# Output product of a gated MLP by Strassen's method, in float32 split into two parts

## The chip, the cores and the metric

The kernel runs on one core of a Trainium2 chip. The core has five engines that work side by side and wait for one another on semaphores: TensorE (PE in the profile, with PEld for its weight loads), VectorE (DVE), ScalarE (ACT), GpSimd (POOL) and SyncE (SP), which here only issues DMAs. TensorE reads SBUF and writes PSUM; DVE and ACT read PSUM and bring results back to SBUF. The metric is the device time of one execution in microseconds (us), as the median of several runs. The host lays out the arrays before and after; this isn't timed.

## The reference

Eight batches of 576 tokens with 8 heads of 64 go through attention in chunks of 64 tokens, and then through a gated MLP with a product along the tokens:

```python
scores = scale * np.matmul(q_c, k_c.transpose(0, 1, 2, 4, 3))   # per batch, head and chunk: 64 x 64
attn = np.exp(scores - np.max(scores, axis=-1, keepdims=True))
attn = attn / (np.sum(attn, axis=-1, keepdims=True) + 1e-09)
x = np.matmul(attn, v_c)                    # with the heads side by side: [8, 576, 512]
h = gelu_tanh(x @ w_in)                     # [8, 576, 1024]
u, v = h[..., :512], h[..., 512:]
v_n = (v - mu) / np.sqrt(var + 1e-06) * g_ln
v_s = np.einsum('ts,bsd->btd', w_sg, v_n) + b_sg[None, :, None]
out = x + (u * v_s) @ w_out                 # w_out: [512, 512]
```

All arrays are float32, w_in and w_out float64 in the host's arrays.

## The kernel before, in words

Every large product is made of three matmuls in place of one: each operand is split into a high part (rounded to fp32r by a copy on ACT) and a low part (the difference, on DVE), and low x high, high x low and high x high are added in one PSUM bank. `split` (L92) makes the two parts; all its copies stand on L94 and all its subtractions on L97.

The program runs attention over 36 tiles of 128 tokens and the MLP over 8 batches of 576. A batch has four stages of units on PE:

- v units (L448, four or five): 12 matmuls of 512 columns each, then gelu on ACT, statistics and normalisation on DVE, and a power on POOL. A fifth unit in even batches takes the 64 odd tokens of two batches. The results lie in the tile `v`.
- u units (L487, four): 24 matmuls of 288 columns, gelu, into the tile `u2`.
- s units (L505, four): the product along the tokens, 28 matmuls; its result times `u2` gives the tile `gt` (L518), which is split into `gh` and `gl`.
- o units (L527, four): 24 matmuls of 288 columns with `w_out`: four blocks of 128 along the depth, three matmuls each, two banks of 288 tokens. DVE adds `xf`, the attention's output (L545), and SP stores `ot` (L546).

Attention has three steps for a tile or a pair: S (scores, L304, with the softmax on DVE, ACT and POOL), T (transposition on DVE with copies on ACT and DVE, L366) and O (product with v, L390, after which `keep`, L423, splits the result into `xh` and `xl` and copies it to `xf`).

The order of the code is written out by hand: `START` (L45) for the first two batches, with a letter and a number for each step, and `SLOTS` (L59) for the later ones, where "8:S78" puts the scores of the tiles 7 and 8 behind the unit with index 8 of a batch. In `START`, L, W and w (and X, x) load and convert w_in, A loads q, k and v up to a tile, Y loads and converts an eighth of w_out (`o_w`, L215, eight steps on ACT and DVE), P and Q are S and O for a pair, G and g load and split w_sg, and D only keeps PE busy. The framework places semaphores and storage. It keeps the code's order as a priority, and puts a later instruction ahead on an engine when the earlier one isn't ready by its estimate.

Storage that matters: PSUM has two banks in `banks` (scores, and early transpositions) and three tiles `pm` of two banks each, which all units and the attention's output share (L455 and others). SBUF has four places `qkv_t` for q, k and v of a tile (L289), which `o_w` uses for staging too; four places `tmp` for `hs`, `blocks`, `gt` and `ot`; one `u2` and one `v`. A tile's load waits until a place is free: q and k in one DMA, v in four DMAs of 64 KB from tile 5 on (L297 to L301).

Of the kernel before, what the change touches and what calls it, by code (L numbers as in the profile page):

```python
# [80 lines left out]
def block_attention_gated_mlp(ctx: ExitStack, tc: tile.TileContext, qkv, w_in, w_out, w_sg, g_ln, b_sg, out):  # L81
# [133 lines left out]
    def o_w(et, half):  # L215
        nonlocal wout_h, wout_l
        if wout_h is None:
            wout_h, wout_l = (w_out_tile(i).rearrange("p (k e) -> p k e", k=KT) for i in range(2))
# [423 lines left out]
```

## Time and profile before

| what | value |
|---|---|
| three runs, median | 515.13 us (514.95 to 515.40) |
| span of the profiled execution | 513.4 us |
| instructions | 12458 |
| mean granted TensorE clock | 0.996 |
| DMA | 46.58 MB, mean 91 GB/s |
| o units, matmuls (L537) | 512 with `gh`, 256 with `gl` |
| waits of PE after 92 us, by the table of waits | none |

The page shows busy time per engine, the span in 40 slices, and the chain of work that ended last: followed back from the last instruction, at each step to what released it. "Idle before" is the time an engine stood before an instruction, with what ended it. PE's busy time rests on modelled ends of matmuls, so its starts are the safer thing to read. In the answers by line, "x32 | 24.1, 755 | 40.3 <-PE pm L514" means 32 instructions, 24.1 us busy, 755 ns for one, and 40.3 us idle before them, mostly until PE's L514 was done. In a timeline the first two columns are the start and the length in us.

### The profile page before, as it was taken

What the parts mean: (1) busy time and instruction counts of PE and PEld (TensorE: products, weight loads), DVE (VectorE), ACT (ScalarE), POOL (GpSimd) and SP (SyncE); (2) the same over time, 40 slices, a digit from 0 to 9 for tenths busy, and PEclk for the clock granted to TensorE, in tenths of its full rate; (3) what the DMA queues carried; (4) which work ended last, traced back from release to release, by engine and by line L of the source; (5) the groups of instructions that cost most, each with busy time, mean ns of one, the idle gap of its engine ahead of it and who ended that gap; (6) DMA issues with size and microseconds to landing.
All of it is one profiled execution on the core that took longest, in us unless ns stands there. A gap on an engine that the chain in (4) does not pass through costs nothing.

```text
span 513.4 us, 12458 instructions
## 1 busy us (share of the span) xinstructions
PE 497.4 (97%) x5278; PEld 461.4 (90%) x5278; DVE 336.9 (66%) x704; ACT 274.3 (53%) x509; POOL 73.7 (14%) x75
## 2 busy tenths in 40 slices
PE   4989999899999999999999999999999999999997
PEld 4577799799999899998999899998999899998996
DVE  6888759986867866577465676578456685536042
ACT  5788667854435775355643766345644666334210
POOL 0123200020110321013100141013100140102000
PEclk9999999899999999999999999999999999999999
DMA  8866001216338404060406204060406300020002
GB/s 333 301 190 196 0 1 43 83 39 178 95 121 234 118 1 126 24 193 2 124 10 184 87 0 126 24 193 2 124 1 193 87 0 3 17 78 0 1 1 92
DMA packets 49595, 46.58 MB, mean 91 GB/s; under 512 B 35202, under 2 KB 39554, under 8 KB 49540
## 3 DMA queue, kind: packets, MB, share of 16 engines
q1 hardware_dynamic: 49540, 45.80, 29.4%
q8 instruction: 41, 0.67, 0.6%
q14 instruction: 14, 0.11, 0.1%
HBM read 36.34 MB, written 9.44 MB: 89 GB/s over the span
## 4 chain that ended last, share of the span: by engine, by line
PE 83%; DVE 7%; ACT 5%; POOL 2%; issue 2%; DMA 1%; DVEq 0%; POOLq 0%; ACTq 0%
PE pm L514 21%; PE pm L537 19%; PE pm L494 19%; PE pm L457 17%; PE pm L415 3%; PE banks L329 3%; POOL sm L466 1%; PE pm L582 1%; DVE nmax L340 1%; DMA wsg<-w_in 1%; ACT ptT L385 1%; ACT ptT L380 1%; POOL xl L97 1%; DVE wsg L133 0%; ACT pt L349 0%
## 5 line engine op out<-in xcount | busy, mean ns | idle before, releaser
L514 PE MATMUL pm<-wsg,v 128*128 128x288 f32 x768 | 108.0, 296 | 0.0
L514 PEld LDWEIGHTS pm<-wsg,v 128*128 128x128 f32 x768 | 103.9, 189 | 0.4
L537 PE MATMUL pm<-gh,wout 128*128 128x288 f32 x512 | 92.3, 297 | 0.0
L537 PEld LDWEIGHTS pm<-gh,wout 128*128 128x128 f32 x512 | 76.1, 189 | 0.5
L363 POOL TENSOR_TENSOR pt<-pt,den 128x512 f32<-128x512 f32 x28 | 30.7, 1111 | 225.3 <-DVE den L362 150.3
L466 POOL TENSOR_TENSOR sm<-sm,neg_half 128x1 f32<-128x1 f32 x36 | 36.3, 1007 | 160.5 <-DVE sm L465 120.2
L494 PE MATMUL pm<-xh,win_l 128*128 128x288 f32 x256 | 55.5, 298 | 1.0 <-ACT win_l L179 1.0
L537 PE MATMUL pm<-gl,wout 128*128 128x288 f32 x256 | 55.5, 296 | 0.0
L94 ACT CAST gh<-gt 128x576 fp32r<-128x576 f32 x32 | 21.5, 673 | 62.8 <-DVE gt L518 62.8
L494 PE MATMUL pm<-xh,win_h 128*128 128x288 f32 x256 | 55.0, 296 | 0.0
L494 PE MATMUL pm<-xl,win_h 128*128 128x288 f32 x256 | 55.0, 296 | 0.0
L457 PE MATMUL pm<-win_h,xl 128*128 128x512 f32 x128 | 52.0, 406 | 0.0
L457 PE MATMUL pm<-win_l,xh 128*128 128x512 f32 x128 | 51.2, 400 | 0.0
L457 PE MATMUL pm<-win_h,xh 128*128 128x512 f32 x128 | 51.1, 399 | 0.0
L518 DVE TENSOR_TENSOR gt<-pm,u 128x576 f32<-128x576 f32 x32 | 24.1, 755 | 40.3 <-PE pm L514 40.3
L545 DVE TENSOR_TENSOR ot<-pm,xf 128x576 f32<-128x576 f32 (+1 forms) x33 | 24.1, 732 | 29.8 <-PE pm L537 29.8
L494 PEld LDWEIGHTS pm<-xh,win_l 128*128 128x128 f32 x256 | 41.4, 188 | 2.4 <-ACT win_l L179 1.4
L537 PEld LDWEIGHTS pm<-gl,wout 128*128 128x128 f32 x256 | 41.5, 189 | 0.0
L494 PEld LDWEIGHTS pm<-xl,win_h 128*128 128x128 f32 x256 | 41.0, 188 | 0.0
L494 PEld LDWEIGHTS pm<-xh,win_h 128*128 128x128 f32 x256 | 41.0, 188 | 0.0
L97 DVE TENSOR_TENSOR xl<-pm,xh 128x512 fp32r<-128x512 f32 (+1 forms) x34 | 21.7, 639 | 26.2 <-ACT xh L94 26.2
L463 DVE BATCH_NORM_STATS2 sm<-hs 128x6 f32<-128x512 f32 x36 | 24.7, 687 | 19.7 <-ACT hs L460 19.5
(121 smaller groups left out, 825.2 us busy)
## 6 DMA issues: line engine op xcount, KB each, us to landing
qkv_t<-qkv SPq DMA_DIRECT2D x32, 512.0 KB, 4.5
out_dram<-ot SPq DMA_DIRECT2D x31, 288.0 KB, 2.2
qkv_t<-qkv SPq DMA_DIRECT2D x124, 64.0 KB, 3.7
qkv_t<-qkv SPq DMA_DIRECT2D x3, 768.0 KB, 9.4
wsg<-w_in SPq DMA_DIRECT2D x4, 512.0 KB, 4.8
wout<-w_in SPq DMA_DIRECT2D x4, 512.0 KB
st<-w_out SPq DMA_DIRECT2D x8, 256.0 KB, 3.5
stage<-w_sg SPq DMA_DIRECT2D x5, 288.0 KB, 3.3
```

The source lines that it names most:

```text
L94: nc.scalar.copy(hi, src)
L97: lo_eng.tensor_tensor(lo, src, hi.bitcast(F32), op=ALU.subtract)
L329: nc.tensor.matmul(sc[o, c, h // 2, :], qt[r, 0, h, :], qt[r, 1, h, :], start=True, stop=True)
L363: (nc.gpsimd if t > last[1] else pick(f"n{t}")).tensor_tensor(pt, pt, den.unsqueeze(2).broadcast_to([P, H, D]), op=ALU.mult)
L457: nc.tensor.matmul(pv, a[:, kt, tok], c[:, kt, DH:], start=(i == 0), stop=(i == 11))
L463: nc.vector.bn_stats(st, h)
L466: nc.gpsimd.tensor_tensor(rs, rs, neg_half, op=ALU.pow)
L494: nc.tensor.matmul(pm[:, j, :HS], a[:, kt, dc], c[:, kt, j * HS : (j + 1) * HS], start=(i == 0), stop=(i == 11))
L514: nc.tensor.matmul(pm[:, j, :HS], a[:, dc], c[:, m, j * HS : (j + 1) * HS], start=(i == 0), stop=(i == len(ops) - 1))
L518: nc.vector.tensor_tensor(gt.rearrange("p (a c) -> p a c", a=2), pm[:, :, :HS], u2[0][:, dt, :].rearrange("p (a c) -> p a c", a=2), op=ALU ...
L537: nc.tensor.matmul(pm[:, j, :HS], a[:, kt, ec], c[:, kt, j * HS : (j + 1) * HS], start=(i == 0), stop=(i == len(ops) - 1),)
L545: nc.vector.tensor_tensor(ot[:, js], pm[:, js, :HS], res[:, js], op=ALU.add)
```

## The change

**Seven products for eight.** For batches 1 to 7 the output product is taken as one of 2x2 blocks: the weights W in blocks of 256 outputs by 256 deep, the gated input G (b11, b12, b21, b22 in the code) in blocks of 256 deep by 288 tokens. With Winograd's form of Strassen's method, S1 = W21 + W22, S2 = S1 - W11, S3 = W11 - W21, S4 = W12 - S2, and T1 = G12 - G11, T2 = G22 - T1, T3 = G22 - G12, T4 = G21 - T2, the products are

- P1 = W11 G11, P2 = W12 G21, P3 = S4 G22, P4 = W22 T4, P5 = S1 T1, P6 = S2 T2, P7 = S3 T3,
- out11 = P1 + P2, out12 = P1 + P6 + P5 + P3, out22 = P1 + P6 + P7 + P5, out21 = P1 + P6 + P7 + P4, each plus its part of x.

A product has 12 matmuls of 288 columns (two halves of outputs, two of depth, three for the split) into one `pm` tile. They run in the order 1, 5, 2, 6, 3, 7, 4. Products 1, 6, 7 and 4 add up in the same tile, 5 and 3 in a second; product 2 has a third. DVE reads a tile between two products. Product 4 comes behind the next batch's first v unit (in batch 7 it has a tile of its own and ends by halves).

```diff
+        if b >= FAST and dt == 1:
+            split(gh[b][:, 0], gl[b][:, 0], b11, nc.scalar, nc.vector)
+            nc.gpsimd.tensor_tensor(b11, b12, b11, op=ALU.subtract)
+            split(gh[b][:, 3], gl[b][:, 3], b11, nc.scalar, nc.vector)
+        if b >= FAST and dt == 3:
+            ts = gs[b] = mp.tile([P, 3, 2, 2, HS], F32R, name="ts", tag="v")
+            nc.vector.tensor_tensor(b11, b22, b11, op=ALU.subtract)
+            split(ts[:, 0, 0], ts[:, 0, 1], b11, nc.scalar, nc.vector)
+            nc.gpsimd.tensor_tensor(b12, b22, b12, op=ALU.subtract)
+            nc.gpsimd.tensor_tensor(b21, b21, b11, op=ALU.subtract)
...
+        if step == 0:
+            o["a"] = new()
+            product(b, 1, o["a"], True)
+            o["r1"] = o_part(o["a"], o_quarter(b, 0, 0))
+            split(ts[:, 1, 0], ts[:, 1, 1], b12, nc.scalar, nc.vector)
+            o["b"] = new()
+            product(b, 5, o["b"], True)
+            o["r5"] = o_part(o["b"], o_quarter(b, 1, 1))
+            split(ts[:, 2, 0], ts[:, 2, 1], b21, nc.scalar, nc.vector)
+        elif step == 1:
+            c = new()
+            product(b, 2, c, True)
+            o_store(b, 0, 0, o_part(c, o["r1"], o["r1"]))
+            product(b, 6, o["a"], False)
+            o["r2"] = o_part(o["a"], o_quarter(b, 0, 1))
+        elif step == 2:
+            product(b, 3, o["b"], False)
+            o_store(b, 0, 1, o_part(o["b"], o["r2"], o["r2"]))
+            product(b, 7, o["a"], False)
+            o_store(b, 1, 1, o_part(o["a"], o["r5"], o["r5"]))
+        elif b < B - 1:
+            product(b, 4, o["a"], False)
+            o_store(b, 1, 0, o_part(o["a"], o_quarter(b, 1, 0)))
+        else:
+            ot = o_part(o["a"], o_quarter(b, 1, 0))
+            d = new()
+            product(b, 4, d, True)
+            for e in range(2):
+                es = slice(e, e + 1)
+                o_part(d, ot, ot, es)
+                o_store(b, 1, 0, ot, es)
...
-        units += [(s_unit, i) for i in range(4)] + [(o_unit, i) for i in range(4)]
+        units += [(s_unit, i) for i in range(4)] + [(o_fast, i) for i in range(3)]
...
             f(b, k)
+            if i == 0:
+                o_fast(b - 1, 3)
```

`new` takes a `pm` tile, `product` issues the 12 matmuls, `o_part` is one DVE addition of 128x576 from PSUM, `o_store` one DMA. The gate's result is written back into `u2` in place of `gt`. In batch 0 the four o units stay, with blocks in another order in storage. T2 to T4 lie in `ts`, which takes the place of `v`.

**Weight sums.** Four new steps K0 to K3 in `START` make S1 to S4 once: `w_whole` adds a block's high and low part on POOL, further POOL additions and subtractions make the sums (eight POOL operations of 128x512 in all), and each sum is split on ACT and DVE. S1 takes the place of W21 after batch 0; the others lie in a new pair of tiles `wx`.

**Separate places for q, k and v.**

```diff
-            qt = att.tile([P, 3, H, D], F32, name="qkv_t", bufs=QKV_BUFS)
+        qks[t] = att.tile([P, 2, H, D], F32, name="qk", tag="qk")
+        nc.sync.dma_start(out=qks[t], in_=qkv[t, :, 0:2])
+        vt = vts[t] = att.tile([P, H, D], F32, name="av", tag="av")
...
     def scores(*tiles):
-        ahead(tiles[-1] + 2)
         att_scores(*tiles)
+        ahead(load_qk, tiles[-1] + 2)
+
+    def outputs(*tiles):
+        att_out(*tiles)
+        ahead(load_v, tiles[-1] + 2)
```

q and k have two places `qk`, v has two places `av`; tiles 2 and 4 lie in `wx`, and tile 3 in `u2` as before. q and k are loaded behind the scores that free their place, v behind the output that frees its own. `o_w` stages in `qk`. `START` gets the new steps and loads:

```diff
-L0 A0 A1 L1 S0 L2 T0 D11 A2 W0 A3 W1 L3 A4 S1 W2 S2 w0 w1 W3 T1 O0 w2 S3 O1 T2 w3 D14 O2 T3 S4 M0 v00 X0 O3 G0 T4 v01
-A8 O4 x0 X1 v02 x1 X2 v03 X3 v04 u00 x2 g0 g1 u01 x3 g2 g3 u02 P5 g4 u03 T5 s00 T6 P7 s01 Q5 s02 T7 T8 s03 Q7 v10 v11
-Y0 v12 Y1 v13 Y2 u10 Y3 u11 Y4 u12 Y5 Y6 u13 Y7 A10 s10 A12 s11 P9 s12 s13 T9 o00 T10 P11 o01 o02 o03 Q9 A14 T11 o10
-T12 o11 Q11 S13 A15 o12 T13 o13
+L0 A0 B0 A1 B1 L1 S0 L2 T0 D11 A2 W0 A3 W1 L3 A4 S1 W2 S2 w0 w1 W3 T1 O0 w2 S3 O1 T2 w3 D14 O2 T3 S4 M0 v00 X0 O3 G0 T4
+v01 A6 B6 O4 x0 X1 v02 x1 X2 v03 X3 v04 u00 x2 g0 g1 u01 x3 g2 g3 u02 P5 A8 g4 u03 T5 s00 T6 P7 s01 Q5 B8 s02 T7 T8
+s03 Q7 v10 v11 Y0 v12 Y1 v13 Y2 u10 Y3 u11 Y4 u12 Y5 Y6 u13 Y7 A10 B10 s10 K0 s11 K1 P9 A12 s12 K2 s13 T9 o00 T10 P11 A14
+o01 o02 o03 K3 Q9 B12 T11 o10 T12 o11 Q11 B14 S13 A15 o12 T13
```

More of the change, by code (lines that the diff above doesn't have):

```diff
@@ L217, in o_w @@
         if wout_h is None:
-            wout_h, wout_l = (w_out_tile(i).rearrange("p (k e) -> p k e", k=KT) for i in range(2))
+            wout_h, wout_l = (blocks_of(w_out_tile(i), 4) for i in range(2))
         n = 2 * P
-        cols, rows = slice(et * P, (et + 1) * P), slice(2 * half, 2 * half + 2)
-        st = att.tile([P, 3 * H * D], I32, name="st", tag="qkv_t", bufs=QKV_BUFS)[:, : 4 * n]
+        rows, blk, cols = slice(2 * half, 2 * half + 2), W_BLOCK[et // 2, half], slice(et % 2 * P, (et % 2 + 1) * P)
+        st = att.tile([P, 4 * n], I32, name="st", tag="qk")
         dst = st[:, : 2 * n].rearrange("p (k c) -> p k c", k=2)
@@ new lines, in s_unit, with g_split @@
+        nc.vector.tensor_tensor(row, pm[:, :, :HS], row, op=ALU.mult)
+        if dt == 0:
+            gh[b] = xp.tile([P, 4, 2, HS], F32R, name="gh", tag=f"big_{b % 2}")
+            gl[b] = xp.tile([P, 4, 2, HS], F32R, name="gl", tag=f"big_{b % 2}")
+        g_split(b, dt)
+    gs = {}
+    def g_split(b, dt):
+        k, two = dt % 2, slice(0, 4, 3) if dt < 2 else slice(1, 3)
+        g = u2[0]
+        row = g[:, dt, :].rearrange("p (a c) -> p a c", a=2)
+        if b < FAST or dt > 1:
+            split(gh[b][:, two, k, :], gl[b][:, two, k, :], row, nc.scalar, nc.vector)
+        b11, b12, b21, b22 = (g[:, 2 * i : 2 * i + 2, j * HS : (j + 1) * HS] for i in range(2) for j in range(2))
+        if b >= FAST and dt == 1:
[8 more added lines that the diff above has]
+            nc.gpsimd.tensor_tensor(b21, b21, b11, op=ALU.subtract)
@@ L541, in o_unit @@
         ot = tmp.tile([P, 2, HS], F32, name="ot", tag="tmp")
         res = xf[b][:, et, :].rearrange("p (a c) -> p a c", a=2)
[L543 to L554 removed]
+        nc.vector.tensor_tensor(ot, pm[:, :, :HS], res, op=ALU.add)
@@ new lines, in o_unit, with product @@
+        nc.sync.dma_start(out=out[b, et].rearrange("p (a c) -> p a c", a=2), in_=ot)
+    os = {}
+    def product(b, n, pm, first):
+        h, l, ts = gh[b], gl[b], gs[b]
+        wh, wl = wout_h, wout_l
+        (ah, al), (ch, cl) = {
+            1: ((wh[:, 0], wl[:, 0]), (h[:, 0], l[:, 0])),
+            2: ((wh[:, 1], wl[:, 1]), (h[:, 1], l[:, 1])),
+            3: ((wx[0][:, 2], wx[1][:, 2]), (h[:, 2], l[:, 2])),
+            4: ((wh[:, 2], wl[:, 2]), (ts[:, 2, 0], ts[:, 2, 1])),
+            5: ((wh[:, 3], wl[:, 3]), (h[:, 3], l[:, 3])),
+            6: ((wx[0][:, 0], wx[1][:, 0]), (ts[:, 0, 0], ts[:, 0, 1])),
+            7: ((wx[0][:, 1], wx[1][:, 1]), (ts[:, 1, 0], ts[:, 1, 1])),
+        }[n]
+        for e in range(2):
+            ops = [(a, c, k) for k in range(2) for a, c in ((al, ch), (ah, cl), (ah, ch))]
+            for i, (a, c, k) in enumerate(ops):
+                nc.tensor.matmul(
+                    pm[:, e, :HS], a[:, k, e * P : (e + 1) * P], c[:, k, :],
+                    start=(first and i == 0), stop=(i == len(ops) - 1), skip_group_check=True,
+                )
@@ L556, in scores, with ahead @@
+    loaded = {load_qk: 0, load_v: 0}
+    def ahead(load, t):
+        while loaded[load] <= min(t, NT - 1):
+            load(loaded[load])
+            loaded[load] += 1
     def scores(*tiles):
-        ahead(tiles[-1] + 2)
         att_scores(*tiles)
+        ahead(load_qk, tiles[-1] + 2)
+    def outputs(*tiles):
+        att_out(*tiles)
+        ahead(load_v, tiles[-1] + 2)
     def att_slots(b, n):
@@ L564, in att_slots @@
             i, what = step.split(":")
-            f = {"S": scores, "T": att_transpose, "O": att_out}[what[0]]
+            f = {"S": scores, "T": att_transpose, "O": outputs}[what[0]]
             tiles = [first[b + b % 2] + int(k, 16) for k in what[1:]]
```

157 lines of the change are left out of this document (95 added, 62 removed).

## The prediction

> **What bounds the kernel now.** I read the page first, for the shares and for the chain that ended last.
>
> ```profile
> PE 497.4 (97%) x5278; PEld 461.4 (90%) x5278; DVE 336.9 (66%) x704; ACT 274.3 (53%) x509; POOL 73.7 (14%) x75
> PE 83%; DVE 7%; ACT 5%; POOL 2%; issue 2%; DMA 1%; DVEq 0%; POOLq 0%; ACTq 0%
> ```
>
> TensorE (PE) is busy for 97% and carries 83% of the chain. Since the end of a matmul is modelled, I then took the busy time by stretches (columns: length, PE, weight load, DVE, ACT, POOL, clock, DMA).
>
> ```profile
> 165.00:281.60 116.60, 116.60 (x1296) 110.43 (x1296) 75.78 (x154) 64.57 (x108) 18.37 (x18) 1.00 0.32 90
> 281.60:398.00 116.40, 116.40 (x1295) 110.23 (x1294) 75.26 (x152) 63.05 (x105) 18.25 (x18) 1.00 0.29 83
> ```
>
> These are two batches each. PE has no gap: a matmul that goes is time gained, and a PE wait that comes is time lost, both in full. The price of a matmul comes from the chain in order of time (batch 7's output product) and from the matmuls of its last unit:
>
> ```profile
> 496.80 12.79 PE pm L537 x96
> 506.37 0.30 PE L537 MATMUL pm<-gl,wout 128*128 128x288 f32 x1
> 509.15 0.29 PE L537 MATMUL pm<-gl,wout 128*128 128x288 f32 x1
> ```
>
> 12.79 us / 96 = 133 ns. The last unit runs one bank to its end and then the other, with other weights at each matmul, as the new products do; 21 matmuls lie between the two rows: 2.78 us / 21 = 132 ns. So neither the accumulation into one bank nor the lost pairing of weights has a price.
>
> **The change part by part.**
>
> *Removed.* A batch has 96 matmuls in its output product now, and 7 x 12 = 84 after. 7 batches x 12 x 133 ns = **11.2 us**, all of it on the path.
>
> *Added on DVE, ACT and POOL.* Prices by form:
>
> ```profile
> L518 DVE TENSOR_TENSOR gt<-pm,u 128x576 f32<-128x576 f32 x32 | 24.1, 755 | 40.3 <-PE pm L514 40.3
> L545 DVE TENSOR_TENSOR ot<-pm,xf 128x576 f32<-128x576 f32 x31 | 23.3, 750 | 27.4 <-PE pm L537 27.4
> L97 DVE TENSOR_TENSOR gl<-gt,gh 128x576 fp32r<-128x576 f32 x32 | 24.5, 767 | 11.3 <-ACT gh L94 10.0
> L94 ACT CAST gh<-gt 128x576 fp32r<-128x576 f32 x32 | 21.5, 673 | 62.8 <-DVE gt L518 62.8
> L97 POOL TENSOR_TENSOR xl<-xf,xh 128x512 fp32r<-128x512 f32 x4 | 5.6, 1410 | 12.4 <-ACT xh L94 12.4
> ```
>
> The last row's idle part says that POOL waited for ACT before them. Per batch: 7 additions from PSUM instead of 4 (3 x 0.750), 7 splits instead of 4 (DVE 3 x 0.767, ACT 3 x 0.673), one subtraction on DVE (0.767) = 5.3 us of DVE and 2.0 of ACT; three subtractions on POOL, which by the 512-wide row cost some 1.41 x 576/512 = 1.6 each. All of the DVE part falls after the gate's last unit. Here are the stretches from there on: output product of an even batch, v and u of the odd one behind it; output product of an odd batch, v and u of the even one.
>
> ```profile
> 211.00:226.00 15.00, 15.00 (x226) 14.76 (x225) 10.29 (x19) 6.46 (x11) 0.63 (x1) 1.00 0.48 139
> 226.00:237.20 11.20, 11.20 (x50) 9.03 (x49) 8.65 (x20) 6.38 (x12) 3.43 (x4) 1.00 0.18 63
> 237.20:252.20 15.00, 15.00 (x226) 14.77 (x225) 9.46 (x20) 9.44 (x15) 1.91 (x2) 1.00 0.38 106
> 267.20:281.70 14.50, 14.50 (x194) 14.43 (x194) 8.52 (x15) 6.05 (x10) 1.05 (x1) 1.00 0.58 171
> 165.40:181.10 15.70, 15.70 (x157) 12.64 (x157) 13.14 (x33) 11.63 (x20) 5.32 (x5) 1.00 0.44 119
> 181.10:193.90 12.80, 12.80 (x101) 12.63 (x99) 7.28 (x15) 9.14 (x16) 1.95 (x3) 1.00 0.00 0
> ```
>
> Even: DVE 10.29 + 8.65 + 5.3 = 24.2 us in 15.0 + 11.2 - 1.6 = 24.6. Odd: 8.52 + 13.14 + 5.3 = 27.0 in 28.6. So DVE becomes 94 to 98% full for some 26 us in each batch; u has 5 us of room behind it. On the average DVE's 336.9 + 37 us are cover enough; at this place the cover is gone, and the question is where PE meets it.
>
> *The new waits.* Batch 7 has no attention beside it and gives the bare chain:
>
> ```profile
> 496.83 0.76 DVE L518 TENSOR_TENSOR gt<-pm,u 128x576 f32<-128x576 f32 x1 [1.48 <-PE pm L514]
> 498.33 0.76 DVE L97 TENSOR_TENSOR gl<-gt,gh 128x576 fp32r<-128x576 f32 x1 [0.74 <-ACT gh L94]
> 497.62 0.67 ACT L94 CAST gh<-gt 128x576 fp32r<-128x576 f32 x1 [3.06 <-DVE gt L518]
> ```
>
> Product, high part, low part end at 499.1; then T2's subtraction to 499.9, its high part (ACT 0.67) to 500.6, its low part to 501.4. Product 6, the fourth in line, starts 36 x 0.133 = 4.8 us after 496.6, at 501.4. This just fits, if DVE does nothing else; the addition after product 1 fits into ACT's 0.7. Before product 7 DVE has ten operations of 0.76 and one wait of 0.74, to 505.2; PE is there 60 x 0.133 = 8.0 us after 496.6, at 504.6: a wait of 0.6. In the batches before, attention's operations stand in between, by the order of the code ahead of the additions. Even: a transposition and its swaps (1.3) before product 6, then a tile pair's split and softmax. Odd: two tiles' splits and a softmax (some 3.8) before the addition after product 1, which product 6 waits for as it adds to that bank. By hand that makes 0.4 to 1.8 us of PE wait, less what other work fills.
>
> The PSUM tiles of L455 are the second wait. One of three stays taken from product 1 until product 4 has been added, behind the next batch's first v unit; that leaves two. In the even batch before:
>
> ```profile
> 217.40 1.16 PE L415 MATMUL pm<-ptT,qkv_t 64*64 64x64 f32 x64
> 221.80 0.59 ACT L437 COPY xf<-pm 128x512 f32<-128x512 f32 x1 [0.76 <-DVE xl L97]
> 224.34 0.75 DVE L545 TENSOR_TENSOR ot<-pm,xf 128x576 f32<-128x576 f32 x1
> 225.93 0.40 PE L457 MATMUL pm<-win_h,xl 128*128 128x512 f32 x1
> ```
>
> Attention's product holds its tile for 5.0 us (217.4 to 222.4), and the addition whose product ended at about 222.6 came 1.7 us later, behind softmax work. With two tiles left, the v unit that follows product 7 can wait for either: 0 to 1.7 us. Behind it on PE stand product 4 and all of v.
>
> From both sides, then, a batch with attention loses between 0 (other matmuls fill each wait, as PE shows no gap now) and some 2.2 us (1.8 plus a part of 1.7). Neither end has the nearer row; I take **0.9**, somewhat below the middle, since scores and v matmuls can move ahead, and 0.6 for batch 7: 6 x 0.9 + 0.6 = **6.0 us**.
>
> *Weight sums and loads.* K0 to K3 are 8 POOL operations (8 x 1.41 = 11.3 us) and four splits, due before batch 1's fast products. Rows for this and for the loads:
>
> ```profile
> 119.00:135.00 16.00, 16.00 (x177) 15.77 (x176) 11.25 (x24) 5.93 (x9) 1.60 (x2) 1.00 0.66 177
> L97 DVE TENSOR_TENSOR wout<-st,wout x8: 407/417/426, 95.6 to 121.2; 128x256 fp32r<-128x256 f32 x8
> 67.46 1.16 PE L329 MATMUL banks<-qkv_t 64*64 64x64 f32 x64
> 75.66 1.16 PE L329 MATMUL banks<-qkv_t 64*64 64x64 f32 x64
> 80.67 1.16 PE L415 MATMUL pm<-ptT,qkv_t 64*64 64x64 f32 x64
> 90.95 1.94 PE L415 MATMUL pm<-ptT,qkv_t 64*64 64x64 f32 x64 [1.46 <-ACT ptT L385]
> qkv_t<-qkv SPq DMA_DIRECT2D x32, 512.0 KB, 4.5
> qkv_t<-qkv SPq DMA_DIRECT2D x124, 64.0 KB, 3.7
> 44.87 2.58 SPq L301 DMA_DIRECT2D qkv_t<-qkv  x4
> ```
>
> POOL has 14 us free in 119 to 135; the weights are ready at 121, the sums are needed at about 150: nothing lost. q and k of tiles 7 and 8 are now loaded after the scores of 5 and 6 (end 68.6): 68.6 + 1 for the issues + 4.5 = 74, before 75.7. Their v goes after the output of 5 and 6 (81.8): two tiles' issues of 2.6 us on SP and 3.7 to land end at 90.7, where PE needs them from 90.95 on. That is level, on a stretch where the profile shows PE waiting: 0 to 1.5 us (the 2.6 of a tile's issues, less the second tile's later turn). w_out's staging has two places in place of four; its last split may come some us after 121, with 13 us to batch 0's product. At the beginning one more issue stands before the second w_in load. Against this stand loads that no longer wait for a whole tile's end. I take 0, range -1 to +2.
>
> *Sum.* 513.4 - 11.2 + 6.0 + 0 = 508.2 us for the profiled execution; the runs' median is 1.7 longer than its span (515.1 against 513.4): **509.9 us**.
>
> **The rivals.**
>
> *Full saving (0.22).* Waits are filled, DVE's room in u takes the rest. For it: no PE gap now, though DVE already runs at 13.14 of 15.70 us in a v stretch. Against it: the ledgers above. 515.1 - 11.2 = 503.9.
>
> *POOL stops DVE (slower, 0.20).* POOL's subtractions of T3 and T4 run just when DVE makes T2 and the splits. The trace shows what such a meeting does:
>
> ```profile
> 41.18 1.59 POOL L97 TENSOR_TENSOR xl<-xf,xh 128x512 fp32r<-128x512 f32 x1 [6.37 <-ACT xh L94]
> 41.63 1.70 DVE L472 SCALAR_TENSOR_TENSOR hs<-hs,sm,g_bc 128x512 f32<-128x512 f32 x1
> L472 DVE SCALAR_TENSOR_TENSOR hs<-hs,sm,g_bc 128x512 f32<-128x512 f32 x36 | 27.8, 773 | 0.0
> ```
>
> The DVE operation took 1.70 us instead of 0.77 and ended 0.6 us after POOL's: it stood until POOL was through. Two such meetings, 0.7 to 0.9 us each, on a DVE that is full would shift product 6 and product 7 in each batch. With the PSUM wait that is some 2.1 us a batch: 7 x 2.1 - 11.2 = +3.5, or 518.6. It decides from 12 x 0.133 = 1.6 us of PE wait a batch. The Trainium skill, "SBUF — State Buffer", section "Who interferes with whom", has this as a rule: a VectorE instruction with two inputs in SBUF and a GpSimd one that reads SBUF block each other for the whole instruction. By that rule all three POOL operations count; the rows above agree with it.
>
> *Given back, no more (0.10).* 1.5 to 1.6 us a batch lost: 514.1 to 516.2, about 515.
>
> *The change isn't what it says.* Were the matmuls slower with new weights each, 84 would have to cost 152 ns to eat it up; the 132 ns exclude that.
>
> **How the numbers follow.** Forecast, partly given back (506 to 513): 0.48; full saving 0.22; given back 0.10; slower 0.20. A measurement of this kernel can tell about 0.2%, 1.0 us. Faster: 0.48 + 0.22 = 0.70; same 0.10; slower 0.20. The range starts at the full saving, 503.9. On top it covers a batch loss of 1.7 us with 1.5 at the start and no more: 515.1 - 11.2 + 7 x 1.7 + 1.5 = 517.3, which leaves out the greater part of the slower case and little below: 0.15 in all.
>
> **What would show it.** Right: 5278 - 84 = 5194 matmuls and 133 ns within each product; DVE over 90% from the gate's end through v; PE gaps of 0.3 to 1.5 us before product 6, product 7 or the first v unit, released by DVE (T2's low part, or an addition); DVE splits stretched to over 1 us where POOL subtracts. Wrong: no PE gap there (full saving); gaps before 92 us or at the outputs of tiles 7 and 8 or 11 and 12, from a DMA (the loads); gaps of over 1.6 us in each batch (slower).

## The result, and the profile after

| | before | after |
|---|---|---|
| median of the runs | 515.18 us (514.95 to 515.40) | 547.42 us (545.34 to 548.87) |
| ratio, 95% interval | | 1.0622 (1.0595 to 1.0649): slower |
| span of the profiled execution | 513.4 us | 544.7 us |
| mean granted TensorE clock | 0.996 | 0.984 |

The forecast was 509.9 us with a range from 503.9 to 517.3. The page of the changed kernel, its busy time, its clock row and its chain:

```profile
PE 498.2 (91%) x5194; PEld 457.4 (84%) x5194; DVE 391.5 (72%) x758; ACT 291.0 (53%) x534; POOL 117.4 (22%) x104
PEclk9999999999888999999998999999998999999999
PE 45%; DVE 27%; ACT 11%; POOL 8%; DMA 3%; issue 3%; SPq 1%; DVEq 0%; POOLq 0%; ACTq 0%
```

84 matmuls are gone, as announced, and PE's share of the chain fell from 83% to 45%: DVE, ACT and POOL now set the end for almost half of the span. The stretches from batch 1's first v unit on, two batches each from the second row (columns as in the prediction):

```profile
92.80:179.50 86.70, 73.84 (x744) 68.75 (x745) 71.18 (x142) 40.18 (x77) 25.75 (x19) 0.94 0.29 87
179.50:304.80 125.30, 116.55 (x1271) 108.87 (x1270) 89.78 (x172) 68.43 (x114) 28.31 (x25) 0.99 0.29 84
304.80:427.10 122.30, 115.89 (x1270) 108.67 (x1269) 88.51 (x168) 67.80 (x113) 27.27 (x24) 0.99 0.27 79
```

The second row was 116.60 us before. For the runs that follow, a finer measure is the time from the first matmul of a batch's u units to that of the next (batch 7: to the end of the last matmul), read from the timeline of PE. It holds each batch's output product whole, with eight block products or seven. "Full saving" is before less 12 x 0.133 = 1.6 us.

| batch | 1 | 2 | 3 | 4 | 5 | 6 | 7 |
|---|---|---|---|---|---|---|---|
| before | 75.3 | 56.15 | 60.22 | 56.15 | 60.22 | 55.21 | 40.66 |
| full saving | 73.7 | 54.55 | 58.62 | 54.55 | 58.62 | 53.61 | 39.06 |
| after | 92.49 | 57.16 | 65.76 | 57.42 | 64.88 | 55.84 | 40.33 |
| e1 loads only | 78.28 | 56.10 | 60.17 | 56.09 | 60.18 | 55.16 | 40.62 |
| e2 subtractions on DVE | 91.14 | 55.77 | 60.16 | 55.77 | 60.16 | 54.10 | 39.58 |
| e8 and sums on DVE | 85.07 | 55.77 | 59.99 | 55.76 | 60.10 | 54.10 | 39.57 |
| e6 sums late | 78.35 | 57.13 | 59.99 | 55.81 | 59.99 | 54.10 | 39.56 |
| e12 halves | 75.79 | 57.48 | 59.31 | 55.89 | 59.31 | 54.37 | 39.07 |
| e18 from batch 3 | 75.96 | 57.00 | 59.42 | 55.87 | 59.33 | 54.35 | 39.06 |

Two places hold the loss. Batch 1 lasts 18.8 us more than the full saving; batches 2 to 7 together 22.4 us more, of which the odd batches 3 and 5 have 13.4. The timeline of batch 3's end shows why, for DVE, ACT, POOL and PE:

```profile
287.36 0.76 DVE L566 TENSOR_TENSOR u<-pm,u 128x576 f32<-128x576 f32 x1
288.15 0.76 DVE L588 TENSOR_TENSOR u<-u 128x576 f32<-128x576 f32 x1
288.26 1.94 POOL L590 TENSOR_TENSOR u<-u 128x576 f32<-128x576 f32 x1 [4.60 <-DVE u L566]
288.86 1.97 DVE L104 TENSOR_TENSOR gl<-u,gh 128x576 fp32r<-128x576 f32 x1
290.24 1.25 ACT L101 CAST ts<-u 128x576 fp32r<-128x576 f32 x2 [1.41 <-POOL u L590]
290.90 1.43 POOL L591 TENSOR_TENSOR u<-u 128x576 f32<-128x576 f32 x1 [0.70 <-DVE gl L104]
290.94 2.67 DVE L104 TENSOR_TENSOR ts<-u,ts 128x576 fp32r<-128x576 f32 x2
291.39 0.58 ACT L101 CAST xh<-pm 128x512 fp32r<-128x512 f32 x1
296.12 0.58 ACT L485 COPY xf<-pm 128x512 f32<-128x512 f32 x1 [0.79 <-DVE xl L104]
296.75 0.61 PE L626 MATMUL pm<-gh,wout 128*128 128x288 f32 x1 [4.49 <-ACT xf L485]
```

The low part `gl` on DVE lasts 1.97 us instead of 0.77: it stands until POOL's subtraction is through. ACT waits in order for POOL's result (1.41 us), and attention's result of tiles 2 and 3, done by PE at 288.4, is copied by ACT only from 291.39 on. Between that copy and the last one, which frees the PSUM tile at 296.7, ACT waits twice more, now for low parts on DVE (1.21 and 0.79 us). Product 2, which needs the tile, stands 4.49 us. That DVE was stretched shows in its sum too: in e2 it has 21 instructions of 0.76 us more and the same busy time (392.0 us against 391.5), so some 16 us of the 391.5 were standing.

In batch 1 the weight sums on POOL do the same to the staging of w_out (rows of DVE and POOL after the change; L138 and L139 last 0.3 us elsewhere):

```profile
127.16 1.28 POOL L243 TENSOR_TENSOR r<-wout,wout 128x512 f32<-128x512 f32 x1 [13.36 <-DVE wout L104]
127.22 1.37 DVE L138 TENSOR_SCALAR st<-st 128x256 f32<-128x256 f32 x1
128.51 1.26 POOL L258 TENSOR_TENSOR r<-r 128x512 f32<-128x512 f32 x1
128.62 1.30 DVE L139 TENSOR_SCALAR st<-st 128x256 int32<-128x256 int32 x1
130.79 0.69 PE L378 MATMUL banks<-qk 64*64 64x64 f32 x32 [2.85 <-DMA qk<-qkv]
```

The last row is a second cost at the start: q and k of tiles 9 and 10 are loaded only when w_out's staging leaves their place, and PE stands at their scores. Behind it come waits for DVE's additions and one more load: PE's gaps of 0.5 us and more in batch 1 are 2.85, 2.67, 1.95, 1.75, 1.76, 0.50 and 1.70 us (the last at 186.4, before the scores of tiles 14 and 15), 13.2 us in all. The rest is for the most part a lower clock of PE behind some of these gaps: it was 0.50 from 136.2 to 139.5, 156.6 to 160.0 and 170.2 to 173.6 us (last section).

### The profile page after: what moved, and what is told of

Read it like the earlier page. It is cut to its first block, busy times and chain, and to the rows that moved or that the text cites. A ratio compares the mean times of both kernels' runs of the same rounds, so it can differ in the third digit from the quotient of the medians.

```text
span 544.7 us, 12453 instructions
## 1 busy us (share of the span) xinstructions
PE 498.2 (91%) x5194; PEld 457.4 (84%) x5194; DVE 391.5 (72%) x758; ACT 291.0 (53%) x534; POOL 117.4 (22%) x104
## 4 chain that ended last, share of the span: by engine, by line
PE 45%; DVE 27%; ACT 11%; POOL 8%; DMA 3%; issue 3%; SPq 1%; DVEq 0%; POOLq 0%; ACTq 0%
PE pm L542 14%; PE pm L505 11%; PE pm L562 8%; PE pm L626 7%; DVE ts L104 3%; POOL u L590 3%; DVE u L566 2%; DVE gl L104 2%; DVE xl L104 2%; POOL sm L514 2%; PE pm L463 2%; DVE nmax L388 2%; DVE pt L399 2%; DVE den L408 1%; DVE v L523 1%
## 5 line engine op out<-in xcount | busy, mean ns | idle before, releaser
L626 PE MATMUL pm<-gh,wout 128*128 128x288 f32 x168 | 39.1, 318 | 11.2 <-ACT xf L485 9.5
L104 DVE TENSOR_TENSOR gl<-u,gh 128x576 fp32r<-128x576 f32 x32 | 32.7, 1030 | 17.2 <-ACT gh L101 17.2
L101 ACT CAST gh<-u 128x576 fp32r<-128x576 f32 x32 | 21.3, 673 | 42.1 <-DVE u L566 30.5
L428 ACT COPY ptT<-blocks 128x512 f32<-128x512 f32 x31 | 19.2, 620 | 43.7 <-DVE blocks L425 31.1
L626 PEld LDWEIGHTS pm<-gh,wout 128*128 128x128 f32 x168 | 30.1, 205 | 12.4 <-ACT xf L485 10.3
L522 ACT ACTIVATE v<-hs,sm 128x512 fp32r<-128x512 f32 x32 | 23.2, 724 | 27.4 <-POOL sm L514 27.2
L566 DVE TENSOR_TENSOR u<-pm,u 128x576 f32<-128x576 f32 x32 | 24.0, 749 | 17.4 <-PE pm L562 17.2
L425 DVE STREAM_TRANSPOSE blocks<-pt 128x512 f32<-128x512 f32 x31 | 21.9, 705 | 15.0 <-POOL pt L411 9.0
```

Of the source, the lines that this page charges most:

```text
L101: nc.scalar.copy(hi, src)
L104: lo_eng.tensor_tensor(lo, src, hi.bitcast(F32), op=ALU.subtract)
L425: nc.vector.transpose(blocks, pt.rearrange("p h t -> p (h t)"))
L428: nc.scalar.copy(ptT, blocks)
L522: nc.scalar.mul(hi, h, rs)
L566: nc.vector.tensor_tensor(row, pm[:, :, :HS], row, op=ALU.mult)
```

## The experiments

All ratios are to the kernel before, with runs of both on the same chip. The theory: POOL's work beside DVE (it stops DVE, and ACT stands behind it) made most of the loss, at the start together with w_out's staging and the loads. Rivals: DVE is simply too full; the PSUM tiles are held too long; the loads alone.

**e1: the loads alone.** No products in blocks, no weight sums; `FAST = 8`, and in the loop `(o_fast, i) for i in range(3)` becomes `(o_unit, i) for i in range(4)`.

> All eight batches use the plain output product (96 matmuls each), product 4 behind the next v unit and the weight sums are left out; the separate places for q, k and v, the new START loads and w_out staged in two places stay. Theory start: the loads cost by themselves what stood before the scores of tiles 9 and 10 after the change, two PE gaps of 2.85 and 2.67 us plus the lower clock behind them, so 515.2 + 6 to 8 = some 522 us. Rival: the start was lost to the weight sums on POOL and to DVE, and the loads cost nothing: 514 to 516 us, with no gap of PE before the scores. After 180 us both expect no gap over 0.3 us apart from one of up to 2 us at 184 us that a load of q and k ended.

Measured: 518.49 us, 1.0072 (1.0057 to 1.0087), between the two expectations. The gaps before the scores are 2.1 and 0.45 us, and batch 1 is 3.0 us longer. The loads cost 3 us, half of what this theory gave them; the steady batches are as before.

**e2: the three subtractions on DVE.**

```diff
-nc.gpsimd.tensor_tensor(b11, b12, b11, op=ALU.subtract)
+nc.vector.tensor_tensor(b11, b12, b11, op=ALU.subtract)
```

and so for `b12` and `b21`.

> The three subtractions of a batch for T1, T3 and T4 run on DVE instead of POOL (3 x 0.77 us a batch, 16 us of DVE in all). Theory POOL: POOL's subtractions, 1.43 to 1.94 us each, stop DVE (the low parts at 1.97 and 2.67 us instead of 0.76) and make ACT wait in order for their results (gh and ts high parts, 11.5 + 10.1 + 5.1 us); without them a batch loses some 2 us less, and the time falls to 530 to 537 us. Rival DVE load: DVE is simply too full behind the gate, 2.3 us more a batch go on PE's wait, and the time rises to 555 to 563 us. Rival PSUM: the gaps come from the tiles held by keep and by product 4, wherever the subtractions run: 545 to 549 us.

Measured: 528.66 us, 1.0262 (1.0247 to 1.0278): 18.8 us less than after the change, with 16 us more of instructions on DVE. Rival DVE load falls; so does rival PSUM as a cause of its own, for the gaps of 4.49 us before product 2 went, and the longest left in odd batches are 1.33 us, before product 6. The gain is larger than the theory's.

**e3: outputs of tiles 2 and 3 before the gate's last unit.** `11:O23` becomes `10:O23`.

> In odd batches the output of attention tiles 2 and 3 of a pair of batches stands one unit earlier, before the gate's last unit instead of behind it; nothing else changes. Theory PSUM: the two gaps of 4.49 us before product 2 at 292 and 414 us, in which PE waited for the PSUM tile that keep held, go, with the lower clock behind them: 547.4 - 9 to 12 = 535 to 538 us. Rival POOL or DVE load: the work of keep only shifts, DVE and ACT stay as late, and another product waits in place of product 2: 544 to 549 us.

Measured: 541.39 us, 1.0513 (1.0475 to 1.0551). Product 2 waits no more, but product 6 does, by 2.16 us: half the gain, as DVE stays late.

**e4: scores of 9 and 10 before w_out's staging.**

```diff
-s02 T7 T8 s03 Q7 v10 v11 Y0
+s02 T7 T8 A10 s03 Q7 B10 v10 P9 v11 Y0
-Y7 A10 B10 s10 K0 s11 K1 P9 A12 s12
+Y7 A12 s10 K0 s11 K1 s12
```

> In START the load of q and k of tiles 9 and 10, their scores and the load of their v stand before w_out's staging instead of behind it, and 11 and 12 are loaded when the staging is through. Theory start: the two gaps of PE at 128 to 136 us (5.5 us) and the lower clock behind them go: 547.4 - 6 to 8 = 539 to 541 us. Rival: the weight sums on POOL and the held tmp places set when batch 1 can go on, and the time saved before 136 us is lost again before 180 us: 545 to 549 us.

Measured: 549.14 us, 1.0662 (1.0644 to 1.0680). The wait moved to the next scores, of tiles 11 and 12, which also waited for their load (5.88 us up to 142.4, 3.06 up to 150.3), and to a unit behind an addition (4.12 us up to 159.2). The time is the rival's within 0.2 us; that POOL's sums set it isn't shown by this run.

**e5: e2 and e3 together.**

> The three subtractions on DVE (528.7 us alone) and the output of the tiles 2 and 3 one unit earlier (541.4 us alone) together. Theory: the steady part is then cured. Two batches take 115.9 us with the subtractions on DVE alone; 116.4 - 2 x 12 x 0.133 = 113.2 us is the full saving. Both visible gaps of 1.33 us (product 6, at 287 and 403 us) go, batches 2 to 7 lose under 2 us in all, and the time is 521 to 525 us; the rest over 504 stands before batch 2. Rival: DVE's load is the limit, the work only moves into other waits, and the time stays at 527 to 530 us.

Measured: 529.18 us, 1.0267 (1.0249 to 1.0286), no change from e2. The two gaps of 1.33 us fell to 0.37, and the batches lasted as long as before: the rival's time, though not yet its reason.

**e8: e5 with the weight sums on DVE** (five lines of `w_whole` and `w_sums` from `nc.gpsimd` to `nc.vector`).

> As the combination of subtractions on DVE and outputs earlier, with the eight weight sums at their old place in START but on DVE instead of POOL. Theory POOL: the POOL sums, 1.27 to 1.79 us each, stretch DVE's operations beside them (1.36, 1.30, 1.79, 1.71 and 2.06 us where 0.25 to 0.77 are usual, some 5 us in all), and eight operations of 0.68 us on DVE cost about the same: the time moves by less than 2 us. Rival: it is the order in which ACT and DVE wait for POOL's results that costs, and the time falls by 4 us or more.

Measured: 522.52 us, 1.0137 (1.0122 to 1.0152): 6.7 us less, the rival's figure. POOL's sums cost more than the DVE time that they stretch. Part of it is the clock: the granted mean rose from 0.988 in e5 to 0.995, and 525.8 x 0.012 - 520.7 x 0.005 = 3.7 us is an estimate of what that was worth.

**e6: weight sums in batch 2, batch 1 plain.**

```diff
-FAST = 1
+FAST = 2
+            if b == FAST:
+                for j in {9: (0, 1), 10: (2, 3)}.get(i, ()):
+                    w_sums(j)
```

K0 to K3 leave `START`; the sums are on DVE.

> As the combination before, but batch 1 keeps the plain output product, and the weight sums are made on DVE in batch 2 beside its product along the tokens. Theory start: of the 14 us that batch 1 loses (85.0 us from its first v unit to that of batch 2, where 72.4 - 1.6 were due) some 10 come from the weight sums and the products of batch 1 on a DVE that is late, so that this stretch takes some 75.4 us, as in the run with the loads alone, and the time is 512 to 515 us (one batch saves less, 1.6 us). Rival: the start is lost to the loads and w_out's staging, and the time stays within 2 us of the combination before. If the sums in batch 2 cost what they cost in batch 1, its two batches become 4 to 10 us longer than 113.2 us.

Measured: 517.67 us, 1.0053 (1.0036 to 1.0070). Batch 1 takes 78.35 us, what e1 has. The sums cost 1.4 us in batch 2 (57.13 against 55.77), not 4 to 10. The time is above the theory's, because the steady batches save little. Their waits are short and stand one behind another, as here in batch 4 on PE, and on DVE beside it:

```profile
336.00 0.29 PE L626 MATMUL pm<-gh,wout 128*128 128x288 f32 x1
336.22 0.44 PE L378 MATMUL banks<-qk 64*64 64x64 f32 x10
336.63 1.83 PE L626 MATMUL pm<-ts,wx 128*128 128x288 f32 x12
338.39 0.69 PE L378 MATMUL banks<-qk 64*64 64x64 f32 x32
339.20 1.16 PE L463 MATMUL pm<-ptT,av 64*64 64x64 f32 x64
```

```profile
335.73 0.75 DVE L637 TENSOR_TENSOR ot<-pm,xf 128x576 f32<-128x576 f32 x1
338.39 0.75 DVE L637 TENSOR_TENSOR ot<-pm,ot 128x576 f32<-128x576 f32 x1
```

Product 6 was due 0.133 us behind 336.00 and came at 336.63, behind the addition that ended at 336.5; scores of another tile filled 0.17 us of it. Attention's output came at 339.20, when the addition from 338.39 had freed its tile.

**e7: w_out staged in `wx`, q and k loaded ahead of it** (from e6).

```diff
-st = att.tile([P, 4 * n], I32, name="st", tag="qk")
+st = const.tile([P, 12 * P], I32, name="st", tag=f"wx_{half}")[:, : 4 * n]
-s03 Q7 v10 v11 Y0
+s03 Q7 A10 B10 v10 v11 Y0
-Y7 A10 B10 s10
+Y7 s10
```

> As the run with the sums late, but w_out is staged in the two tiles of the weight sums, free until then, and q and k of tiles 9 and 10 are loaded ahead of it. Theory loads: PE finds q and k when it comes to the scores, the two gaps of 2.1 and 0.45 us go, and the 3.0 us that the loads alone cost between the first v units of batches 1 and 2 (75.4 against 72.4 us) go with them: some 3 us less than the run before, 509 to 512 us, faster than the kernel before the change. Rival: those 3 us are w_out's staging in two places in place of four, which DVE gets to late, and the time is that of the run before within 1 us.

Measured: 516.66 us, 1.0027 (1.0016 to 1.0039): only 1.0 us. The two gaps went and batch 1 fell to 76.01 us, but w_out's steps, now possible at 70 us, went ahead of the softmax of tiles 5 and 6, and batch 0 became 2.1 us longer.

**e11: POOL for nobody.** e5 and, behind the three subtractions:

```diff
+            for _ in range(2):
+                nc.gpsimd.tensor_tensor(b22, b22, b12, op=ALU.subtract)
```

> The combination of subtractions on DVE and outputs earlier (529.2 us), and in addition two subtractions of 128x576 on POOL behind the gate of each batch from 1 on, whose results nothing uses: no instruction of ACT, and of PE none before the next batch's u units, waits for them. Moving POOL's three subtractions to DVE gained 18.8 us, 2.7 us a batch. Theory lock: DVE stands while POOL subtracts, 2 x 1.4 us a batch at the place where it is full, and the gain goes again: 539 to 549 us, with DVE operations of 1.4 to 2.7 us there. Rival order: the gain came from ACT, which no longer stands in order behind POOL's results; nobody waits for these, and the time stays at 528 to 532 us.

Measured: 540.01 us, 1.0478 (1.0461 to 1.0496): 10.8 us more, for results that nothing uses. That is DVE standing behind POOL, the lock of the expectation, by itself: in the trace no instruction waits for these two, and POOL's own next work isn't held up by them (it stands idle for 5.64 us first, last row). In batch 3, DVE and POOL:

```profile
292.46 0.75 DVE L104 TENSOR_TENSOR ts<-u,ts 128x576 fp32r<-128x576 f32 x1
292.62 3.75 POOL L593 TENSOR_TENSOR u<-u 128x576 f32<-128x576 f32 x2 [17.15 <-DVE gl L104]
293.13 1.98 DVE L591 TENSOR_TENSOR u<-u 128x576 f32<-128x576 f32 x1
295.03 0.68 DVE L388 TENSOR_REDUCE nmax<-banks 128x8 f32<-128x512 f32 x1
295.63 0.74 DVE L639 TENSOR_TENSOR ot<-pm,xf 128x576 f32<-128x576 f32 x1
302.01 1.05 POOL L411 TENSOR_TENSOR pt<-pt,den 128x512 f32<-128x512 f32 x1 [5.64 <-DVE den L410]
```

L591, with both inputs in SBUF, takes 1.98 us instead of 0.75; the addition that reads PSUM takes 0.74 in the midst of POOL's second operation, which ends at 296.4. So in these rows the operands decide. The Trainium skill, "SBUF — State Buffer", section "Who interferes with whom", limits the contention to VectorE instructions with two SBUF inputs or in a 2-port mode; both rows agree with it. L591 takes 1.98 us in each of the seven batches: 7 x 1.23 = 8.6 us of the 10.8. After the change DVE stood some 16 us, with three subtractions. What remains of e2's 18.8 us, some 8, is this longer standing and ACT's place behind POOL's results; the two were not told apart.

**e9: attention ahead of the gate** (from e7).

```diff
-9:T3 10:O23 11:S4 13:T4
+9:T3 10:O23 10:S4 14:T4
-8:S78 11:T7 12:T8 14:O78 14:S9A
+8:S78 9:T7 10:T8 11:O78 11:S9A
-                split(dst[0], dst[1], src, nc.scalar, nc.vector)
-                nc.scalar.copy(dst[2], src)
+                nc.scalar.copy(dst[0], src)
+                nc.scalar.copy(dst[2], src)
+                nc.vector.tensor_tensor(dst[1], src, dst[0].bitcast(F32), op=ALU.subtract)
```

> As the run with w_out staged apart (516.7 us), but attention's steps that stood behind the gate (scores, transpositions and outputs of two tiles in each batch) stand before its last unit, and the copy to xf comes ahead of the low part, so that the PSUM tile is free earlier. With the subtractions on DVE and no gap of PE over 0.4 us, a batch with attention still lasts 55.8 and 60.0 us from u unit to u unit where the full saving gives 54.6 and 58.6. Theory ledger: this 1.2 to 1.4 us a batch is PE waiting in steps of 0.2 to 0.6 us before products 6, 7 and the next v unit, for DVE, on which attention's operations stand between the new ones, and for the tile that keep holds; it goes for the most part, and the time is 510 to 513 us. Rival: DVE's sum of work is what counts, wherever it stands, and the time stays at 515 to 518 us.

Tile 4's transposition comes one unit later. Measured: 533.41 us, 1.0355 (1.0330 to 1.0379): far worse than both theories said. PE stands 2.53 us for ptT before an output at 211 us, and 6.6 us in all, six times, for high parts of `ts`: beside the s units there is no room for all of attention, and the gate's results came later. The run changes two things at once, the places and the order of the copy. The ledger theory (DVE's work summed up against the time it has) is neither shown nor hit by it, but moving work this way is no remedy.

**e10: e9 with half of the subtractions before the gate's last unit.**

```diff
+        if b >= FAST and dt > 1:
+            t11, t12, t21, t22 = (a[:, k] for a in (b11, b12, b21, b22))
+            nc.vector.tensor_tensor(t11, t22, t11, op=ALU.subtract)
+            if dt == 2:
+                nc.vector.tensor_tensor(t12, t22, t12, op=ALU.subtract)
+                nc.vector.tensor_tensor(t21, t21, t11, op=ALU.subtract)
```

> As the run before, and the subtractions for T2, T3 and T4 are made by halves of depth, the first halves beside the gate's last unit, so that some 1.0 us of DVE less stands behind it. Theory ledger: what PE still waits there becomes shorter in each batch, batch 7 too, which has no attention and loses 0.5 us (39.58 us from its u units to the last matmul where 39.06 would be the full saving): 0.3 to 0.8 us a batch, 2 to 4 us in all, 507 to 511 us. Rival: with attention out of the way the waits are gone already or hang on the chain through ACT, and the time is that of the run before within 1 us.

The three subtractions behind the last unit do only their second halves now. Measured: 532.38 us, 1.0337 (1.0322 to 1.0353), the rival's time. Batch 7, without attention, reached the full saving, 39.07 us; the others, in sum, stayed as in e9 within 1.1 us.

**e12: the halves alone** (e7 with e10's edit).

> As the run with w_out staged apart (516.7 us), attention where the change has it, and only the subtractions for T2, T3 and T4 made by halves of depth, the first halves beside the gate's last unit: some 1.0 us of DVE less behind the gate. Theory ledger: in batch 4 of the run with the sums late PE stood some 0.3 us each before product 6, before attention's output and before the next v unit, each behind a DVE operation in a row without a gap from 330 to 340 us; with that row shorter by 1.0 us the first two go, batch 7 gains 0.5 us, and the batches fall by 0.5 to 0.9 us each: 512 to 514 us. Rival tile: the next v unit's wait for the tile of attention's output is the one that counts, the others only shift into it, and the time is 515.5 to 517.5 us.

Measured: 514.83 us, 0.9992 (0.9984 to 1.0001): level with the kernel before, and between the two expectations. Against e7, batches 3 and 5 gain 0.7 us each and batch 7 0.5; the even ones lose 0.1 to 0.4.

**e13: e12, the copy in `keep` first as in e9, and other first loads.**

```diff
-L0 A0 B0 A1 B1 L1 S0
+L0 A0 A1 L1 B0 B1 S0
```

> As the run before; the copy to xf comes before the low part in keep, so that the PSUM tile is free some 0.6 us earlier; and in START the second part of w_in is loaded ahead of v (the first u unit of batch 0 began 1.1 us later after the change than before it, 54.6 against 53.5 us). Theory: the start gives back 1.0 us, even batches 0.3 to 0.5 us each at the next v unit, three of them: 2 us less than the run before, 510 to 512 us, faster than the kernel before the change. Rival: ACT's row sets the release of the tile, not the order of the two, and only the start's 1 us comes.

Measured: 517.35 us, 1.0045 (1.0032 to 1.0057), worse than both theories said. Batches 2 to 6 are 0.2 to 0.7 us longer each, and the first u unit comes 2 us later, behind a gap of 1.76 us at 40 us that ended with a copy to xf. So the order of copy and low part doesn't free the tile to any use; why it harms wasn't followed.

**e14: e13 with w_out's steps one unit later.**

```diff
-v11 Y0 v12 Y1 v13 Y2 u10 Y3 u11 Y4 u12 Y5 Y6 u13 Y7
+v11 v12 Y0 v13 Y1 u10 Y2 u11 Y3 u12 Y4 Y5 u13 Y6 Y7
```

> As the run before, with w_out's eight steps one unit later each in START. Staged apart, their work on ACT and DVE came at 70 us, among the softmax of tiles 5 to 8, and PE stood 1.56 and 0.84 us before attention's output at 82 and 94 us. Theory: later steps leave DVE to attention, one or both gaps go, and the time falls by 0.8 to 2 us. Rival: the steps are taken as soon as their data is there, whatever their place in the code, and the time is that of the run before within 0.5 us.

Measured: 517.84 us, 1.0055 (1.0041 to 1.0068): batch 1 1.0 us shorter, batch 2 0.4 longer, and the time is that of e13.

**e15: e12 with the later steps.**

> The run with halves (514.8 us) with w_out's eight steps one unit later in START, and neither the changed copy nor the changed first loads, which together cost 2.5 us. In the run that had all of them the stretch of batch 1 was 1.0 us shorter (75.16 us against 76.14). Theory: this 1.0 us comes through, 513.5 to 514.2 us. Rival: it was given back at the next batch's weight sums (58.06 against 57.64 us), and the time is 514.4 to 515.2 us.

Measured: 514.83 us, 0.9994 (0.9985 to 1.0003): the rival.

**e16: other order of the products** (from e15); the additions and stores go with their products.

```diff
         elif step == 1:
             product(b, 2, c, True)
-            product(b, 6, o["a"], False)
+            product(b, 3, o["b"], False)
         elif step == 2:
-            product(b, 3, o["b"], False)
-            product(b, 7, o["a"], False)
-        elif b < B - 1:
-            product(b, 4, o["a"], False)
+            product(b, 6, o["a"], False)
+        else:
+            product(b, 7, o["a"], False)
+            product(b, 4, d, True)
```

> As the run before, with the products in the order 1, 5, 2, 3, 6, then behind the next batch's first v unit 7 and 4, product 4 in a tile of its own. Product 6 has 1.6 us more and product 7 4.4 us more before PE comes to them. Theory order: the waits of 0.3 to 0.5 us before product 6, before attention's output and before the next v unit go, 0.5 to 1.2 us in each batch with attention: 507 to 511 us. Rival: DVE is behind by a fixed amount of work, the waits move to the next v and u units, whose results now come behind 24 matmuls of the batch before, and the time is 513 us or more.

Measured: 520.33 us, 1.0099 (1.0084 to 1.0115). In batches 2 to 5 product 6 waits no more (product 3 does, by up to 0.78 us). But the v unit behind batch 2 and that behind batch 4 wait 1.16 us each for the copy of attention's output, since product 7's tile is still held then. In these batches the PSUM tiles are the limit; whether another order would save something with more of them was not tested.

**e17: w_out's first two steps in the places of q and k** (from e12): for `et == 0` `o_w` takes its place under the tag `qk` again, and `START` reads

```diff
-s03 Q7 A10 B10 v10 v11 Y0 v12 Y1 v13
+s03 Q7 B10 v10 v11 Y0 v12 Y1 A10 v13
```

> The run with halves (514.8 us), with w_out's first two steps staged in the places of q and k, which come free only behind the scores of tiles 7 and 8, and the other six in the tiles of the weight sums. Theory: w_out's first two steps on ACT and DVE come at 80 us again, the gap of 1.57 us at 82 us goes, q and k of tiles 9 and 10 are still there in time, and the time is 512.5 to 513.8 us, below the kernel before. Rival: the steps staged apart are taken at 70 us in their place, and the time stays at 514.3 to 515.3 us.

Measured: 514.58 us, 0.9993 (0.9984 to 1.0003). A gap of 1.56 us is still there, up to 83.1 us: the rival.

**e18: e17 with batch 2 plain.**

```diff
-FAST = 2
+FAST = 3
-            if b == FAST:
-                for j in {9: (0, 1), 10: (2, 3)}.get(i, ()):
+            if b in (2, 3):
+                for j in ({9: (0, 1), 10: (2,)}, {9: (3,)})[b - 2].get(i, ()):
```

> As the run before, with the plain product in batch 2 as well, so that only batches 3 to 7 save, and the last weight sum made in batch 3. Batch 2 took 57.48 us in the run with halves, 1.33 more than before the change (56.15). Theory: this excess goes for the most part, since without the new products DVE has the sums' room: some 1 us less than the run before. Rival: the sums cost the same wherever they stand, and batch 3 becomes longer by what batch 2 gains: within 0.5 us of the run before.

Batch 2 gets its four plain o units, and the step in batch 3 adds W21 and W22 anew. Measured: 514.14 us, 0.9984 (0.9975 to 0.9992): the fastest of all, and the rival's time. Its interval lies just below 1, but 0.16% is less than the 0.2% named in the prediction. Batch 2 gained 0.5 us. Three of the four sums still cost 0.85 us in a plain batch (57.00 us against 56.15).

## Why the prediction was wrong

**The account.** By the table of batches, 513.4 - 11.2 + 18.8 + 22.4 = 543.4 us; 0.9 us more lie ahead of batch 1's u units and 0.4 behind the last matmul, which makes the 544.7 measured. The forecast had 0 for the start and 6.0 for the waits of all seven batches.

**Removed: right.** 5194 matmuls, 0.133 us apart within products. In e12 batch 7 lasts 39.07 us, the whole saving.

**"I take 0, range -1 to +2" for the start: wrong, the largest miss.** Batch 1 lost 18.8 us. From the runs' batch 1: the loads 3.0 (e1), the subtractions on POOL 1.4 (after to e2), the sums on POOL some 5.7 (e5, 90.75, to e8, 85.07). Of the rest, e6 took away 6.7 by moving the sums, now on DVE, and keeping batch 1 plain (with 1.6 us more of matmuls); these two were not told apart. The step that failed is "POOL has 14 us free in 119 to 135; nothing lost": I counted POOL's free time and not what POOL takes from DVE, though the row of 1.70 us stood in the same text. "Some us after 121" for w_out's last split was 132.6, and I had not asked what is loaded into its places behind it: q and k of tiles 9 and 10, for which PE stood 2.85 and 2.67 us.

**"6 x 0.9 + 0.6 = 6.0" for the waits: the mechanism stood, its cover didn't.** Without POOL (e8) batches 2 to 7 lose 1.2, 1.4, 1.2, 1.5, 0.5 and 0.5 us, 6.3 in all where 5.1 was forecast for these six. That DVE's work behind the gate makes waits is shown by batch 7, where doing half of the subtractions before the gate's last unit gave its 0.5 back. That the sum comes so close to the price is in part luck: e8 has the three subtractions on DVE, and the ledger was too high. For odd batches it added the v stretch of batch 2 (13.14 us of DVE), which stands behind batch 1, to the output product of batch 3. The v stretch that follows batch 3 has less:

```profile
281.70:297.30 15.60, 15.60 (x157) 12.57 (x156) 11.14 (x26) 10.51 (x17) 3.70 (x4) 1.00 0.24 72
```

8.52 + 11.14 + 5.3 = 25.0 us in 28.5, 88% and not 94. With POOL the loss is 22.4 us. So "three subtractions on POOL", 1.6 us each at no cost to DVE, was the wrong line.

**The rival "POOL stops DVE": right in mechanism and sign, too small.** It priced 2.1 us a batch and nothing for the start; measured were 22.4 / 6 = 3.7 in batches 2 to 7, and 18.8 in batch 1, of which the runs put 1.4 and 5.7 to POOL. It took 0.7 to 0.9 us for a meeting and two meetings; `gl` alone was held for 1.2 us, `ts` by another 1.2, and two things came behind it that were not in the price. ACT waits in its order for POOL's results:

```profile
ACT gh L101 <- POOL u L584: 11.5, 7, 2.3
ACT ts L101 <- POOL u L590: 10.1, 7, 1.7
ACT ts L101 <- POOL u L591: 5.1, 7, 0.9
PE pm L626 <- ACT xf L485: 9.5, 3, 4.5
```

(columns: us in all, times, longest). And in odd batches what ACT holds up is the tile that product 2 needs: the wait for PSUM tiles was expected at the v unit behind product 7, 0 to 1.7 us, and came at product 2 with 4.5.

**The clock was not in the sum.** 544.7 x (1 - 0.984) = 8.7 us against 513.4 x (1 - 0.996) = 2.1: some 6.6 us of the loss are slow matmuls behind the gaps (below). This is an estimate: it takes PE as busy all the time that its clock was low.

**The signs named ahead.** DVE's parts over 1 us where POOL subtracts: seen. Gaps before product 6 released by DVE: seen (0.67 us in batches 2, 4 and 6). DVE over 90% from the gate's end through v: not seen; from there to the next u unit it is 27.11 of 34.70 us in batch 3 (78%), and without POOL, in e8, 21.96 of 25.70 and 24.74 of 28.70 (85 and 86%). Where the rest of the 24.2 us of even batches went was not followed. Without a gap it runs for some 10 us only (e6, 330 to 340 us). Gaps of over 1.6 us "in each batch" as the sign of slower: only in odd batches; in even ones gaps of 0.3 to 0.7 us stand in a row. Gaps at the outputs of 7 and 8 or 11 and 12 for the loads: not seen; they were at the scores of 9 and 10 and of 14 and 15.

**What stays open.** In e12 and e18 batch 4 still loses 1.3 us, and odd batches lose 0.7. It is not the DVE work before product 6 alone (e12); another order of the products only moved the wait to the PSUM tiles (e16). START still has 2 us that e14, e15 and e17 didn't find.

## What to carry to other kernels

POOL's free time is not free where DVE is the engine that is late. Here a DVE operation with two inputs in SBUF stood until the POOL operation beside it was through (1.2 us each time), and ACT stood where its next instruction used POOL's result (up to 2.3 us). When an engine off the bottleneck has no gap in a stretch, price every addition there by what stands in order behind it, up to the buffer that the bottleneck needs next. And give the start of a kernel, where every engine is full, a ledger of its own before calling anything there free.

## What the runs showed of the hardware

After some gaps PE ran at half speed for a while. In e3 product 6 came after a gap of 2.16 us (timeline, then stretches with the clock in the third column from the end):

```profile
296.75 3.22 PE L626 MATMUL pm<-ts,wx 128*128 128x288 f32 x12 [2.16 <-DVE ot L637]
```

```profile
286.00:294.00 8.00, 7.98 (x86) 7.52 (x85) 5.47 (x8) 4.69 (x8) 2.65 (x2) 1.00 0.49 131
296.80:300.00 3.20, 3.20 (x14) 3.20 (x15) 3.20 (x7) 0.57 (x1) 0.00 (x0) 0.52 0.00 0
300.00:304.00 4.00, 4.00 (x29) 3.82 (x29) 3.01 (x7) 1.86 (x4) 1.04 (x1) 1.00 0.32 112
```

12 matmuls took 3.0 us (296.75 to 299.77) instead of 1.6: the gap cost 1.4 us more than itself. After the change the gaps of 4.49 us were followed by clocks of 0.55 and 0.56 over 3.5 us; in e6, with no gap over 0.7 us after 135 us, the mean clock is 1.000. The Trainium skill, "TensorE: Matmul & The Clock Gate", section "What's actually happening", gives half rate after an idle window of about 3.4 us; here 2.16 us were enough.

The length of a gap alone doesn't decide. After the change the clock stayed full behind the gap of 2.85 us that ended at 130.79 (first row) and fell to half behind one of 1.95 us that ended at 155.94 (second row); in e1 and e6 it stayed full behind 2.09 and 1.95 us. What decides was not followed.

```profile
130.80:134.20 3.40, 2.72 (x46) 2.42 (x46) 2.63 (x6) 1.08 (x2) 1.55 (x2) 1.00 0.11 17
156.60:160.00 3.40, 3.40 (x17) 3.40 (x16) 3.34 (x7) 1.99 (x4) 0.00 (x0) 0.50 0.72 241
```
